# Layer 1 of a retention and two-layer feed-forward kernel: four directly multiplied weight blocks instead of eight, six pairs by seven products instead of four

## The chip, the cores and the metric

One Trainium2 chip, one core. The metric is the device time of one execution in microseconds (us), and lower is better. MB and GB/s count 10^6 and 10^9 bytes; the KB of the profile's DMA lists are 1024 bytes.

## The reference

Retention (attention with a decaying mask and no softmax) over 4 batches, 8 heads, 576 positions and 64 dimensions a head, then two feed-forward layers on the 2304 x 512 result:

```python
ret = scale * (q @ k.T) * Dmat          # Dmat = gamma ** (i - j) for i >= j, else 0
x = merge_heads(ret @ v)                # 2304 tokens x 512
h = x @ w_in;  g = h * cos(h);  x = g @ w_out                       # layer 1
h = x @ w2_in; g = max(h, 0) + log1p(exp(-abs(h))); y = g @ w2_out  # layer 2
```

w_in is 512 x 2048 and w_out 2048 x 512. The weights come as 64-bit words and are turned into float32 on the chip. Every float32 product is done as three matmuls of a high and a low part (high x high, high x low, low x high).

## The kernel before, in words

A weight block is 128 of the 2048 hidden features, so a layer has 16 (`NF`). A pair is two of them.

**Retention.** 32 pieces (`front`, `masks`, `states`, `back`, `after`), one for a head pair and a part of a batch. The first 16 run alone, the other 16 are spread over the first three token groups of layer 1 (`SPREAD`). Their results x are kept in SBUF as high and low parts and stored to DRAM (`xdh`, `xdl`).

**Layer 1, first part** (`moe_a`, `slot`, `out1`). Blocks 0 to `FA` - 1 have their weights resident (tiles `wh`, `wl`, made by `weight`). Tokens go in five groups (512, 512, 384, 384, 512 columns). For each group and block: 12 matmuls from x into a PSUM bank (L798), the activation h cos h on ScalarE and VectorE (`activate`), its two parts `gh` and `gl`, and 12 matmuls into four accumulators (L897). The partial result of a group goes to DRAM (`pd`).

**Layer 1, second part** (`quad`, `unit`). The other blocks are taken in pairs, over three chunks of 768 tokens, each two halves of 384 columns. A quad is one pair and one chunk: the product of two feature blocks, two halves of the model dimension and two halves of the tokens is done in seven products of 6 matmuls (L1002) on sums and differences of the operands, where straight multiplication takes eight. `x_load` makes the seven x operands of a chunk (three of them from sums on VectorE or GpSimd), `weight_in` the seven weight operands of a pair (tile `pair`). Bank copies (`cv`, `c5`) and adds on VectorE put the seven products together. A `unit` is the output product of one pair and one half chunk: 24 matmuls (L1353). After a pair's last unit GpSimd adds the result to `pd` in DRAM by an accumulating DMA.

**Layer 2** (phases 1 and 2 of the loop over `ph`) is done in pairs throughout, four pairs a phase; its out product too goes by seven products (`unit_s`, L1131). Its in-weights stand in two slots: a pair is made from the converted weights (`wd` in DRAM) for the first chunk, stored to `wpd`, and read back for the others (`weight_in_s`). The chunks run through the pairs forwards and backwards by turns (`turn`), so that two pairs need no load.

**Weights.** `convert` loads one block's half (512 KB), and ScalarE and VectorE turn it into float32. `convert_ahead` stores the result to `wd`; `load_values` and `weight_in_s` read it.

**The order of the work.** Nothing is ordered on the chip. Every operation is handed to `Plan` with an engine, a planned duration and a key (the time at which it is wanted). `Plan.order` picks, again and again, the operation that can start first on its engine (ties by key), lets some operations go to one of two engines, and so fixes one order for each engine. The some 40 constants at the top move keys. All loads and stores but the accumulating ones are issued by SyncE (SP in the profile), in one order: a DMA whose buffer is not ready holds up those behind it.

## Time and profile before

| | |
|---|---|
| median of 3 runs (lowest, highest) | 843.84 us (843.11, 844.63) |
| the profiled execution, its span | 841.66 us, 839.9 us |
| busy TensorE (PE), VectorE (DVE), ScalarE (ACT), GpSimd (POOL) | 98%, 77%, 65%, 9% of the span |
| granted TensorE clock | full in all 40 slices of the page |
| DMA | 174.69 MB, 208 GB/s over the span |

The page gives busy times of engines; a matmul's own duration is longer than its share of the time, because matmuls overlap. What a matmul costs in a dense stretch is the distance between starts, which the chain of waits shows.

### The profile page before, as it was taken

Reading aid. Unit: us, or ns where it says so; the run is one execution under the profiler, and the core shown is the slowest. Engines: PE = TensorE matmul, PEld = TensorE weight load, DVE = VectorE, ACT = ScalarE, POOL = GpSimd, SP = SyncE. Lnnn points to the kernel's source line nnn. Section 1 sums busy time; section 2 is a strip of 40 time slices with the busy share of each in tenths; the row PEclk is TensorE's granted clock in tenths of the full one; section 3 lists DMA queues with packets and bytes.
Section 4 is the critical chain, followed back from the end, with each engine's and each line's share of the span. In section 5 each row is a group of like instructions: output and inputs, shape, how many; then the busy total and the mean of one; then the engine's idle time right before and its main releaser. Section 6 shows DMA issues by size and latency. Waiting matters only on the chain.

```text
span 839.9 us, 15626 instructions
## 1 busy us (share of the span) xinstructions
PE 824.0 (98%) x5732; PEld 773.7 (92%) x5732; DVE 649.5 (77%) x1441; ACT 548.2 (65%) x1189; POOL 72.6 (9%) x94
## 2 busy tenths in 40 slices
PE   7999999999999999999999999999999999999996
PEld 5767877899988999999999998999999999999996
DVE  3789765655894798769877689779698998876786
ACT  1379664756875888879987675564565765555442
POOL 3531000100021000111011010000000000000000
PEclk9999999999999999999999999999999999999999
DMA  9698878747594134776787477617477683555222
GB/s 318 263 361 267 310 251 284 252 142 235 158 325 134 64 113 151 201 225 196 202 245 266 122 223 267 224 65 262 151 248 274 237 309 139 189 207 201 88 76 76
DMA packets 67292, 174.69 MB, mean 208 GB/s; under 512 B 6160, under 2 KB 28560, under 8 KB 65168
## 3 DMA queue, kind: packets, MB, share of 16 engines
q1 hardware_dynamic: 63760, 168.98, 57.2%
q0 software_dynamic: 3456, 4.72, 3.8%
q8 instruction: 45, 0.74, 0.3%
q14 instruction: 31, 0.25, 0.1%
HBM read 110.76 MB, written 62.91 MB: 207 GB/s over the span
## 4 chain that ended last, share of the span: by engine, by line
PE 88%; DVE 6%; DMA 2%; issue 2%; ACT 1%; SPq 0%; POOL 0%; DVEq 0%; POOLq 0%; ACTq 0%
PE acc L1131 19%; PE ha L1002 16%; PE acc L897 12%; PE acc L1353 11%; PE s L1002 8%; PE hb L798 4%; PE ha L798 4%; PE hb L1002 4%; PE o L711 2%; DMA raw<-in_qkv 1%; PE o L798 1%; PE s L798 1%; PE s L634 1%; DVE x L314 1%; DMA dq_t<-in_dq 1%
## 5 line engine op out<-in xcount | busy, mean ns | idle before, releaser
L1002 PE MATMUL ha<-x,pair 128*128 128x384 f32 x864 | 174.7, 336 | 1.2 <-ACT cv L318 0.6
L1002 PEld LDWEIGHTS ha<-x,pair 128*128 128x128 f32 x864 | 149.4, 188 | 3.7 <-DVE x L314 1.2
L1131 PE MATMUL acc<-pair,gh 128*128 128x256 f32 x576 | 113.3, 283 | 0.0
L1353 PE MATMUL acc<-gh,pair 128*128 128x384 f32 x384 | 105.5, 335 | 0.0
L1131 PEld LDWEIGHTS acc<-pair,gh 128*128 128x128 f32 x576 | 89.5, 191 | 0.5 <-ACT gh L1112 0.3
L1131 PE MATMUL acc<-pair,ah 128*128 128x256 f32 x432 | 86.7, 282 | 0.5 <-DVE pt L1210 0.5
L1002 PE MATMUL s<-x,pair 128*128 128x384 f32 x432 | 86.8, 335 | 0.0
L1131 PE MATMUL acc<-pair,gl 128*128 128x256 f32 x288 | 81.7, 284 | 0.7 <-DVE gl L314 0.7
L1002 PEld LDWEIGHTS s<-x,pair 128*128 128x128 f32 x432 | 75.6, 188 | 0.4 <-DVE pair L314 0.2
L1131 PEld LDWEIGHTS acc<-pair,ah 128*128 128x128 f32 x432 | 70.0, 190 | 0.7 <-DVE pt L1210 0.7
L1353 PEld LDWEIGHTS acc<-gh,pair 128*128 128x128 f32 x384 | 70.1, 188 | 0.3 <-ACT pt L318 0.2
L1353 PE MATMUL acc<-gl,pair 128*128 128x384 f32 x192 | 64.1, 334 | 0.0
L1131 PE MATMUL acc<-pair,al 128*128 128x256 f32 x216 | 61.1, 283 | 0.3 <-DVE al L314 0.3
L897 PE MATMUL acc<-gh,wh 128*128 128x512 f32 (+1 forms) x160 | 60.2, 377 | 0.3 <-ACT gh L876 0.3
L897 PE MATMUL acc<-gl,wh 128*128 128x512 f32 (+1 forms) x160 | 59.1, 369 | 0.3 <-DVE gl L314 0.3
L897 PE MATMUL acc<-gh,wl 128*128 128x512 f32 (+1 forms) x160 | 58.9, 368 | 0.0
L841 ACT ACTIVATE er<-er 128x384 f32<-128x384 f32 (+1 forms) x88 | 48.3, 551 | 16.2 <-DVE er L837 15.8
L847 ACT ACTIVATE er<-er,hp_t 128x384 f32<-128x384 f32 (+1 forms) x88 | 56.4, 641 | 1.1
L1131 PEld LDWEIGHTS acc<-pair,gl 128*128 128x128 f32 x288 | 55.0, 191 | 1.5 <-DVE gl L314 1.5
L1112 ACT ACTIVATE gh<-sf 128x512 fp32r<-128x512 f32 x72 | 45.3, 632 | 16.3 <-DVE sf L1086 7.5
L318 ACT ACTIVATE cv<-ha 128x384 f32<-128x384 f32 x72 | 35.4, 491 | 31.5 <-PE ha L1002 31.0
L314 DVE TENSOR_TENSOR gl<-sf,gh 128x512 fp32r<-128x512 f32 x72 | 49.5, 689 | 6.4 <-ACT gh L1112 4.8
(215 smaller groups left out, 1851.1 us busy)
## 6 DMA issues: line engine op xcount, KB each, us to landing
wr<-in_w SPq DMA_DIRECT2D x64, 512.0 KB, 4.9
wpd<-pair SPq DMA_DIRECT2D x8, 1792.0 KB, 6.9
pair<-wpd SPq DMA_DIRECT2D x8, 1792.0 KB, 6.9
wd<-wk SPq DMA_DIRECT2D x40, 256.0 KB, 2.8
sd<-x SPq DMA_DIRECT2D x12, 768.0 KB, 3.7
x<-sd SPq DMA_DIRECT2D x12, 768.0 KB, 6.4
raw<-in_qkv SPq DMA_DIRECT2D x12, 640.0 KB, 6.3
x<-pd SPq DMA_DIRECT2D x18, 384.0 KB, 5.1
```

The costliest lines, as they stand in the source:

```text
L314: e.tensor_tensor(out_, a, hi.bitcast(F32), ALU.subtract)
L318: nc.scalar.activation(out_, in_, AF.Copy)
L634: nc.tensor.matmul(X()[j][:, z], k_(j, z), q_(z)[Z[j]], start=True, stop=True)
L711: nc.tensor.matmul(o_at(z)[Z[j]], lhs(j), rhs(j), start=start, stop=stop, skip_group_check=True)
L798: nc.tensor.matmul(h_[:, 0:n], lhs, rhs[:, d, 0:n], start=(k == 0), stop=(k == 3 * NC - 1))
L841: nc.scalar.activation(e["r"], e["r"], AF.Abs)
L847: nc.scalar.activation(e["r"], e["r"], AF.Sin, bias=hp_t[:, 0:1], scale=-1.0)
L897: nc.tensor.matmul(acc[o][:, 0:n], l[:, s], e[r], start=(first and z == 0), stop=(last and z == 2))
L1002: nc.tensor.matmul(R(r), w_(a), x_(b), start=(start and n == 0), stop=(n == 5), skip_group_check=True)
L1112: nc.scalar.activation(T[hk], T[fk], AF.Copy)
L1131: nc.tensor.matmul(acc[m][:, i * 256:i * 256 + 256], l[p], r[o], start=(s == 0 and i == 0 and n == 0), stop=(s == half_p - 1 and n == 2), ...
L1353: nc.tensor.matmul(acc[m][:, 0:HN], l[:, z_], e[r], start=(first and z == 0), stop=(last and z == 2))
```

## The change

The first part keeps four blocks (`FA` 8 to 4). The second part has six pairs (`P0`), numbered from `FQ[0]` = 2. Their in-weights use the two-slot ring that layer 2 had, now in a pool of its own (`pp`): for the first chunk a pair is made from `wd` and stored to `wpd`, and later chunks read it back. So all twelve of these blocks are converted ahead and stored, where two pairs were converted in place before. The last token group's four blocks (`moe_a(NM - 1, job)`, spaced by `OFF`) are laid among the first quads. Product operands and groups are the same in both layers now. `c5` is gone: the copy of product 5 goes into the first half of `cv`, and `cv` has one buffer instead of two. `weight_in` is removed; other tiles move between pools. The constants are other numbers.

```diff
-FA = 8
+FA = 4
-FS = 5
+FS = 2
...
-XHOME = "qqqqrrrpp"
+XHOME = "qqqqqqqpp"
...
+    pp = pool("pp", 1, side="right")
-    wpd = dram.tile([128, 8, 3584], F32, name="wpd")
+    wpd = dram.tile([128, NF, 3584], F32, name="wpd")
...
-    MB = t_ + 1.0
+    P0 = (NF - FA) // 2
+    NQ = (P0, half_p, half_p)
+    FQ = (FA // 2, 0, half_p)
-    CM = [MB - TIE]
+    CM = [M[-1] - TIE]
+    MB = M[-1] + OFF[-1] + LL + 6.0
     for ph in range(3):
-        CM.append(CM[-1] + nb * half_p * UC[ph])
+        CM.append(CM[-1] + nb * NQ[ph] * UC[ph])
...
-        q = turn(y, s) + (ph - 1) * half_p if ph else half_p + s
+        q = FQ[ph] + turn(ph, y, s)
...
-                if name == "5":
-                    c["5"] = wp["q"].tile([128, HN], F32, tag="c5", name="c5", bufs=2)
-                elif z == 0:
-                    c["v"] = wp["q"].tile([128, 2, HN], F32, tag="cv", name="cv", bufs=2)
-                copy(eng, c["5"] if name == "5" else c["v"][:, z], R(r))
+                if name != "5" and z == 0:
+                    c["v"] = wp["q"].tile([128, 2, HN], F32, tag="cv", name="cv", bufs=1)
+                copy(eng, c["v"][:, z], R(r))
...
-        op(ACT_DVE, both, K + 3 * DT - EARLY, keep(3, 0, "5"), r=[rk[3], ("qopen",)], w=[(c5,)], new=[("c5", 2, c5)])
+        op(ACT_DVE, both, K + 3 * DT - EARLY, keep(3, 0, "5"), r=[rk[3], ("qopen",)], w=[(cv, 0)])
...
-            nc.vector.tensor_tensor(R(4), R(1), c["5"], ALU.add)
+            nc.vector.tensor_tensor(R(4), R(1), c["v"][:, 0], ALU.add)
...
-        key = KI(ph, y, s) - (W[0] if y == 0 and s < 2 else W[1])
+        key = KI(ph, y, s) - (W[0] if y == 0 and s < 2 else W[1] if y == 0 or ph else XW)
         def make():
-            p = wp[HOME[slot_]].tile([128, 3584], F32R, tag=f"pair{slot_}", name="pair")
+            p = pp.tile([128, 3584], F32R, tag=f"pair{slot_}", name="pair")
...
-    for i, (layer, q) in enumerate([(1, half_p + 2), (1, half_p + 3)] + [(2, q) for q in range(half_p)]):
-        convert_ahead(layer, q, M[1] + CA[0] + 4 * i * CA[2], CA[2])
-    for q in range(2):
-        k = M[NM - 2] + W2[0] + W2[1] * q
-        job(k, weight_in, 1, half_p + q, k, W2[3], False)
-        job(k + 0.1, weight_out, 1, half_p + q, k + 2 * W2[3], W2[3], False)
+    moe_a(NM - 1, job)
+    for i in range(P0):
+        k = M[0] + CA[0] + 4 * i * CA[2]
+        job(k, convert_ahead, 1, FQ[0] + i, k, CA[2])
+    for q in range(NP2):
+        k = CM[0] + CA[1] + 4 * q * CA[3]
+        job(k, convert_ahead, 2, q, k, CA[3])
```

The orders, read from the two programs. In them and in the trace, `x` is an operand of a chunk or a group, `pair` a pair's weights, `wr` the raw words of a block's half, `wk` its float32 value, `raw` the input of a retention piece, and `acc` an accumulator; a number behind a name is a buffer. In the changed program the helper of all SP rows has line 309 (306 before), the first part's products L757 and L856 (L798 and L897 before), the quads' L963 (L1002 before).

TensorE before, where the first quad begins (`x_2435` and `x_2438` are operands of the first chunk, `pair_2433` is the first pair's weights, `acc2` and `acc3` belong to the last token group):

```order
L897 MATMUL acc2_2998<-gh_3107,wl_1000 128x512
L897 MATMUL acc3_3026<-gh_3107,wh_999 128x512
L897 MATMUL acc3_3026<-gl_3110,wh_999 128x512
L897 MATMUL acc3_3026<-gh_3107,wl_1000 128x512
L1002 MATMUL ha_3167<-x_2435,pair_2433 128x384 x6
L1002 MATMUL hb_3187<-x_2438,pair_2433 128x384 x6
L897 MATMUL acc0_2983<-gh_3144,wh_1043 128x512
```

Two products of the quad stand together, and after them the last group goes on. By then the first part lacks only the out products of the last group's last three blocks.

TensorE in the change, at the same quad (`x_1955` to `x_1961` are the first chunk's seven operands, `pair_129` the first pair's weights, `x_1542` the last group's x):

```order
L856 MATMUL acc2_2007<-gh_2040,wl_794 128x384
L963 MATMUL ha_2087<-x_1955,pair_129 128x384 x6
L856 MATMUL acc3_2100<-gh_1934,wh_707 128x384
...
L757 MATMUL o_2166<-x_1542,wh_707 128x512 x2
L757 MATMUL o_2166<-x_1542,wl_708 128x512
L963 MATMUL hb_2186<-x_1958,pair_129 128x384 x6
L963 MATMUL s_2199<-x_1956,pair_129 128x384 x6
L963 MATMUL ha_2087<-x_1959,pair_129 128x384 x6
L963 MATMUL s_2199<-x_1957,pair_129 128x384 x6
L963 MATMUL ha_2087<-x_1960,pair_129 128x384 x6
L856 MATMUL acc0_2251<-gh_2240,wh_707 128x512
```

One product stands alone, then come 38 rows of the first part (30 of the fourth group, the first product of the last group), then five products in a row. The last group, which was almost done before, has only begun here.

SyncE before, where the first chunk's operands are loaded:

```order
L306 DMA wr2_2742<-in_w1 128x1024
L306 DMA wr0_2762<-in_w1 128x1024
L306 DMA xdh_95<-x_1355 512x1x384
L306 DMA xdl_96<-x_1355 512x1x384
L306 DMA wr1_2802<-in_w1 128x1024
L306 DMA x_2435<-xdh_95 128x2x384
L306 DMA x_2435<-xdl_96 128x2x384
L306 DMA x_2436<-xdh_95 128x2x384
L306 DMA x_2436<-xdl_96 128x2x384
```

SyncE in the change, where the first chunk's operands are loaded:

```order
L309 DMA wr0_1916<-in_w1 128x1024
L309 DMA wd_103<-wk_1930 128x512
L309 DMA x_1955<-xdh_98 128x2x384
L309 DMA x_1955<-xdl_99 128x2x384
L309 DMA x_1956<-xdh_98 128x2x384
L309 DMA x_1956<-xdl_99 128x2x384
...
L309 DMA x_1958<-xdh_98 128x2x384
L309 DMA x_1958<-xdl_99 128x2x384
L309 DMA wr1_2037<-in_w1 128x1024
L309 DMA wpd_104<-pair_129 128x3584
L309 DMA wpd_104<-pair_130 128x3584
```

The loads follow raw words and converted halves directly, as before, and behind them come the stores of the first two pairs' seven operands (1.84 MB each), which were not there.

SyncE in the change, at the fourth pair of the second part (`pair_2495`); nothing like it stands in this stretch of the order before:

```order
L309 DMA wr2_2386<-in_w1 128x1024
L309 DMA wd_103<-wk_2425 128x512
L309 DMA wr_2453<-wd_103 128x2x512
L309 DMA wpd_104<-pair_2287 128x3584
L309 DMA pair_2495<-wd_103 128x512
L309 DMA pair_2495<-wd_103 128x2x256
L309 DMA wd_103<-wk_2499 128x512
L309 DMA wr_2525<-wd_103 128x2x512
L309 DMA wd_103<-wk_2527 128x512
L309 DMA wr_2542<-wd_103 128x2x512
L309 DMA wr_2560<-wd_103 128x2x512
```

The load of the fourth pair's weights stands behind the store of the third pair's, which waits for that pair's operands to be made, and behind all that was issued before: by the shapes of the rows 67.1 MB through the second load of `pair_2495`. Over the whole program SP issues 203.0 MB in the change and 169.0 MB before; TensorE has 288 matmuls of 512 columns where it had 576, and 2820 of 384 where it had 2472.

## Rows read from the trace of the kernel before

**Rows 1.** The page, its head and section 1: busy us, share of the span.

```profile
span 839.9 us, 15626 instructions
...
PE 824.0 (98%) x5732; PEld 773.7 (92%) x5732; DVE 649.5 (77%) x1441; ACT 548.2 (65%) x1189; POOL 72.6 (9%) x94
```

**Rows 2.** Waits of TensorE, whole span: us in total, times, longest us.

```profile
PE acc L639 <- POOL raw L604: 2.8, 2, 2.3
PE hb L1388 <- DVE er L1380: 1.5, 1, 1.5
PE s L634 <- DVE st L693: 1.0, 1, 1.0
...
PE ha L1002 <- ACT cv L318: 0.6, 1, 0.6
```

**Rows 3.** The chain of waits: start us, us, what.

```profile
62.66 2.72 PE ha L798 x12
...
168.33 2.08 PE ha L798 x12
...
345.54 4.16 PE acc L1353 x24
```

**Rows 4.** Timeline of TensorE: first block's product, then first quad's; start us, us.

```profile
48.96 0.72 PE L798 MATMUL ha<-x,wh 128*128 128x512 f32 x2
...
273.91 1.23 PE L1002 MATMUL ha<-x,pair 128*128 128x384 f32 x6
```

**Rows 5.** Windows: busy time of each engine, clock, DMA's busy share and rate.

```profile
core 0: us, PE busy (x) PEld busy (x) DVE busy (x) ACT busy (x) POOL busy (x), PEclk, DMA share, GB/s
0.00:45.00 45.00, 39.70 (x590) 29.99 (x592) 25.45 (x89) 10.66 (x34) 20.51 (x37) 1.00 0.81 299
45.00:115.00 70.00, 68.44 (x466) 54.26 (x462) 57.89 (x121) 58.52 (x116) 12.58 (x16) 1.00 0.87 309
45.00:190.00 145.00, 143.44 (x1047) 116.87 (x1042) 100.89 (x219) 103.43 (x210) 19.83 (x26) 1.00 0.75 264
50.00:60.00 10.00, 9.39 (x79) 6.70 (x78) 8.93 (x18) 9.24 (x20) 4.15 (x5) 1.00 1.02 411
220.00:240.00 20.00, 20.00 (x113) 19.49 (x112) 19.60 (x38) 16.98 (x33) 2.78 (x3) 1.00 0.68 233
560.00:600.00 40.00, 40.00 (x287) 40.00 (x286) 33.84 (x76) 22.20 (x54) 0.00 (x0) 1.00 0.51 188
```

**Rows 6.** ACT and DVE by line and shape: busy us, mean ns of one, idle before.

```profile
L1228 ACT ACTIVATE pair<-tt 128x768 fp32r<-128x768 f32 x8 | 6.8, 846 | 0.1
L1251 DVE TENSOR_TENSOR tt<-pair 128x256 f32<-128x256 f32 x24 | 9.5, 418 | 0.0
L314 DVE TENSOR_TENSOR pair<-tt,pair 128x768 fp32r<-128x768 f32 x8 | 7.6, 954 | 0.3
L318 ACT ACTIVATE c<-s 128x384 f32<-128x384 f32 x36 | 17.6, 490 | 4.1 <-PE s L1002 3.9
L1025 DVE TENSOR_TENSOR hb<-hb,cv 128x384 f32<-128x384 f32 x36 | 20.2, 562 | 5.2 <-ACT cv L318 3.1 <-ACT gh L876 1.0 <-PE hb L1002 0.9
```

**Rows 7.** DMA of the page: issues, KB each, median us from issue to landing.

```profile
wpd<-pair SPq DMA_DIRECT2D x8, 1792.0 KB, 6.9
pair<-wpd SPq DMA_DIRECT2D x8, 1792.0 KB, 6.9
```

**Rows 8.** Timeline of SP: two reads of the ring in layer 2.

```profile
521.09 0.32 SPq L306 DMA_DIRECT2D pair<-wpd  x1
...
535.23 0.32 SPq L306 DMA_DIRECT2D pair<-wpd  x1
```

More of the change, by code (lines that the diff above doesn't have):

```diff
@@ L512, in weight_out @@
-    def weight_out(layer, q, key, step, ahead):
-        slot_ = q % half_p
-        wk = ("wo", layer, q)
-        made = (wk, "made")
-        def make():
-            p = wp[HOME[slot_]].tile([128, 2048], F32R, tag=f"po{slot_}", name="pair")
+            p = wp[POH[slot_]].tile([128, 2048], F32R, tag=f"po{slot_}", name="pair")
             T[wk] = p.rearrange("p (j g d) -> p j g d", j=2, g=2)
-        op("host", 0.0, key, make, r=[(HOME[slot_] + "open",)], w=[made], new=[(f"wo{slot_}", 1, wk)])
-        if ahead:
-            oks, ovs = load_values(layer, q, 1, key)
+        op("host", 0.0, key, make, r=[(POH[slot_] + "open",)], w=[made], new=[(f"wo{slot_}", 1, wk)])
@@ L524, in weight_out @@
+        oks, ovs = load_values(1, q, 1, key)
         for j in range(2):
-            k = key + j * step
-            ok, ov = (oks[j], ovs[j]) if ahead else convert(layer, 2 * q + j, 1, k)
+            k = key + j * W3[4]
+            ok, ov = oks[j], ovs[j]
             op("act", t_act(512), k + 2.2, lambda j=j, ov=ov: nc.scalar.activation(T[wk][:, j, 0], ov(), AF.Copy),
@@ L1043, in made @@
                 if gk not in T:
-                    a = place(half_p * y + s, t, j)
-                    T[gk] = stash()[:, a:a + HN]
+                    n = P0 * y + s
+                    a = place(n, j)
+                    T[gk] = stash()[:, a:a + HN] if t else first_g(n, j)
                 return T[gk]
@@ L1300, in make @@
         def make():
-            if s < 2:
-                p = wp[HOME[2 + s]].tile([128, 3584], F32R, tag=f"pair{2 + s}", name="pair")
+            if s == 0:
+                p = wp["q"].tile([128, 3584], F32R, tag="ox", name="pair")
                 T[wk] = p[:, 0:1792], p[:, 1792:3584]
             else:
-                z = 2 * s - 4
-                T[wk] = tuple(wp[HOME[z + g]].tile([128, 2048], F32R, tag=f"po{z + g}", name="pair")[:, 0:1792] for g in range(2))
-        op("host", 0.0, key, make, w=[made], new=[(f"wp{2 + s}", 1, wk)] if s < 2 else [(f"wo{2 * s - 4 + g}", 1, wk) for g in range(2)])
+                z = 2 * s - 2
+                T[wk] = tuple(wp[POH[z + g]].tile([128, 2048], F32R, tag=f"po{z + g}", name="pair")[:, 0:1792] for g in range(2))
+        i_ = op("host", 0.0, key, make, w=[made], new=[(f"wo{2 * s - 2 + g}", 1, wk) for g in range(2)] if s else [("ox", 1, wk)])
+        if ph == 1 and s == 0:
+            first_out.append(i_)
         r_, t_ = (lambda i: (i, False)), (lambda i: (i, True))
@@ L1344, in unit @@
                 ak = ("acc", 0, y, t, m)
-                first, last = s == 0 and j == 0, s == half_p - 1 and j == 1
+                first, last = s == 0 and j == 0, s == P0 - 1 and j == 1
                 def mo(m=m, j=j, e=e, first=first, last=last):
@@ L1578, in retention_moe_moe @@
             job(k, x_load, ph, y, k)
-            for s in range(half_p):
+            for s in range(NQ[ph]):
                 job(KI(ph, y, s), quad, ph, y, s)
+                job(KI(ph, y, s) - max(0.1, W[0] if y == 0 and s < 2 else W[1] if y == 0 or ph else XW), weight_in_s, ph, y, s)
                 if not ph:
@@ L1608, in retention_moe_moe @@
             plan.ops[i][4].update(plan.users[last_wr[2]])
-        for t in range(2):
+        for n in range(P0, nb * P0):
             for j in range(2):
-                for s in range(half_p):
-                    a = place(half_p * (nb - 1) + s, t, j)
-                    if a < 512 * m + 512 and a + HN > 512 * m:
-                        plan.ops[i][4].update(plan.users[gof(0, nb - 1, s, t, j)])
+                a = place(n, j)
+                if a < 512 * m + 512 and a + HN > 512 * m:
+                    plan.ops[i][4].update(plan.users[gof(0, n // P0, n % P0, 1, j)])
+    for i in first_out:
+        for n in range(P0, nb * P0):
+            for j in range(2):
+                plan.ops[i][4].update(plan.users[gof(0, n // P0, n % P0, 0, j)])
     plan.emit(nc)
```

224 lines of the change are left out of this document (96 added, 128 removed).

## The prediction

> **What bounds the kernel now.** I read the engines' busy time first: TensorE is busy for 824.0 us of 839.9 [rows 1]. Then its waits: the longest in total is 2.8 us, the ones on the second part's bank copies 0.6 us [rows 2], so what TensorE has to do sets the time, and the other engines and the DMA queues lie beside it. A change that takes work from TensorE gains just that, as long as nothing else becomes late. So there are two questions: how much work goes, and whether what feeds TensorE still comes in time where it is moved together.
>
> **What TensorE saves.** In a dense stretch 12 matmuls of 512 columns take 2.72 us, so one takes 0.2267 us; 12 of 384 columns take 2.08 us and 24 take 4.16 us, 0.1733 us each, in the first part and in the second [rows 3]. Four blocks leave the first part. By the two orders that is 288 matmuls of 512 columns and 192 of 384: 65.3 + 33.3 = 98.6 us. Two pairs come into the second part, three chunks each: 2 x 3 x (42 + 48) = 540 matmuls of 384 columns, 93.6 us. The saving is **5.0 us**. It is less than the 36 spared products' 6.2 us, since the second part uses 384 columns at 0.451 ns a column where groups of 512 cost 0.443. The 32 retention pieces and all of layer 2 keep their matmuls.
>
> **What comes onto the other engines.** Six pairs instead of four give 6 quads more, with 18 copies on ScalarE and 18 adds on VectorE; four blocks less give 20 activations less against the 24 of the new quads. VectorE has 1486 instructions for 1441, ScalarE 1211 for 1187. Over the span neither matters at 77% and 65% [rows 1]. It matters where they come together. The busiest 20 us of VectorE before were 19.60 us of 20, and TensorE lost nothing there [rows 5]. In the change, from the first block of the fourth group to the first product of the fourth pair, TensorE has 228 matmuls of 384 and 96 of 512 columns and a piece and a half of retention, some 65 us. VectorE has 124 instructions there. At 0.478 us (57.89 us for 121) to 0.516 us (19.60 us for 38) each [rows 5] they take 59 to 64 us. That fits, barely. Before, the stretch from 45 to 115 us, with VectorE at 57.89 of 70 us and ScalarE at 58.52, cost TensorE 1.56 us [rows 5]. I bound this term at 0 to 3 us, twice that, and take 0, the busiest window being the nearer case; its cover is gone if VectorE also has to wait for loads.
>
> The shared buffer adds a wait. Product 5's copy now waits for the add that reads the first copy; behind the copy wait product 3, which writes the same bank, and so TensorE. From product 2's end to product 3's start there are two products, 2.08 us; the add takes 0.56 us and the copy 0.49 us [rows 6], which leaves 1.03 us. If the add finds VectorE in an operation of 768 columns (0.95 us), nothing is left for the signals between engines. I take 0, since the order puts the adds early, and at most 0.1 us in each of 18 quads, 2 us; a gain is excluded, since a wait is only added.
>
> The ring of two costs nothing by itself: layer 2 runs on it before, reads of 1.84 MB are 14 us apart there [rows 8] and land 6.9 us after issue [rows 7], and TensorE is busy for 40.00 of 40 us [rows 5]. A quad with its two units takes 42 + 48 matmuls, 15.6 us, so the second part gives as much room.
>
> **What comes onto the DMA queue, the uncertain term.** SP issues 203.0 MB instead of 169.0 over the span: six pairs' operands are stored and eight times read back, 14 x 1.84 MB, and four pairs' halves go through DRAM. More important is when. Before, TensorE starts its first block at 48.96 us and its first quad at 273.91 us [rows 4]; between them lie 540 matmuls of 512 and 384 of 384 columns, 189.0 us, so 36.0 us are retention and small losses. The same 36.0 us stand in the change, whose order is the same up to that first block. Its first quad then starts at 48.96 + 36.0 + 192 x 0.2267 + 162 x 0.1733 = 156.6 us. The fourth pair's first product comes after 288 and 318 matmuls, at **205.3 us**. Its operands were loaded at most some 4 us before: three sums of 0.42 us and the pass of 768 columns on ScalarE (0.85) and VectorE (0.95) are 3.1 us [rows 6], the rest waits for a turn. So the load must land by 201.3 us. In SP's order 67.1 MB stand up to and with that load. By 45 us, 45 x 299 GB/s = 13.5 MB had been moved [rows 5], by rows that are the same in both programs up to 11 MB. So **53.6 MB in 156 us, 343 GB/s without a pause.** The second chunk's first operands ask for the same: 83.6 MB by 250 us.
>
> The queue before never had to do that. From 45 to 115 us it moved 309 GB/s at a share of 0.87, from 45 to 190 us 264 at 0.75 [rows 5]: 352 to 355 GB/s of busy time. Raw words and inputs alone went at 411 [rows 5]. At 355 GB/s without a pause the load lands at 196 us and nothing is late. At 309, the rate of the best long stretch, it lands at 218.5 us and the quad is 17.2 us late. Between these I take 338 GB/s, 0.96 of 352, nearer to the upper end, because the pauses before were a queue with nothing to send, and now there is always something behind: landing at 203.6 us, **2.3 us late**. By the same rate the second chunk's operands land at 252.4 us, 2.3 us late again, which the first delay already covers. Later the demand falls: the first read-back, 89.1 MB, is wanted at 281 us, 320 GB/s.
>
> The Trainium skill, page "DMA: Bandwidth & Descriptors", section "Bandwidth", gives 425 GB/s for one core alone with 16 MB in one transfer and 341 with 1 MB, measured on loads issued from GpSimd. With 425 the load would land at 171 us and all 5.0 us would be kept; with 341 it would land at 202.2 us, 0.9 us late. This trace has 411 GB/s for large reads and 352 for the mixture, so I go by the trace.
>
> **The sum.** -5.0 + 2.3 + 0 + 0 = -2.7 us. The profiled execution took 841.66 us, so 839.0 us for one like it; the median of the runs, 843.84, stands 2.2 us above it, and from that the prediction is **841.1 us**. 0.2% is 1.7 us, about what a measurement of this kernel can tell.
>
> **Rivals.**
> *The DMA queue sets the pace of layer 1's start (slower).* The place is the load of the fourth pair, then the second chunk's operands. For it: 343 GB/s are wanted for 156 us, within 3% of the best mixed rate, and SP issues in order, so one store that waits holds up all loads. Also, writes and short rows have a larger part than before. Against it: the load has 4 us to spare at the rate of the busy time. It decides from 332 GB/s on, where the delay eats all 5.0 us. At 320 GB/s the delay is 11.2 us and the time 850 us, at 309 it is 17.2 us and 856 us.
> *Nothing is late (faster by all of it).* For it: at 352 GB/s the load is in time, and the ring has worked in layer 2. Against it: a queue with no pause for 156 us, which no stretch shows. The time is 843.8 - 5.0 = 838.8 us; if part of the 1.56 us that TensorE lost around 45 to 115 us goes too, 838.
> *Given back in small pieces (no change).* VectorE at 59 to 64 of 65 us, the shared buffer and the queue take 3.3 to 6.7 us together: 842.1 to 845.5 us. For it: three resources are nearly full in the same 60 us. Against it: VectorE at 98% cost nothing before.
>
> **How the numbers follow.** The forecast, with 1 to 3.3 us given back, gets 0.33, nothing late 0.14, the small pieces 0.20, the DMA bound 0.33. So faster 0.47, same 0.20, slower 0.33. The range starts at 838, where all is kept and a little more, and goes to 851, beyond the 850 us of 320 GB/s; that leaves out some 0.04 below and 0.12 above. The likeliest side's own range is 838 to 842.1.
>
> **What would show it.** Right: 5206 matmuls with the counts above; the first quad near 156 us and the fourth pair's first product within 3 us of 205; the DMA share over 0.93 from 45 to 200 us; waits of TensorE on pair or x of some 2 us in the quads' first chunk; later none on `cv`. Wrong: TensorE idle by over 5 us between 150 and 260 us with DMA or a late operand as releaser, which is the first rival; or waits on VectorE of some us in the fourth and last groups; or many short waits of product 3 on the copy, which would make the shared buffer the cost; or dense matmuls at another distance, which would upset the 5.0 us.

## The result and the profile after

Over 12 runs the changed kernel takes 846.67 us (845.19 to 848.93); the kernel before took 842.12 us in 12 runs beside it. The ratio is 1.0054, 95% interval 1.0041 to 1.0067: **0.54% slower**, some 4.5 us. The forecast was 2.7 us faster. The profiled execution (`after` below), 848.93 us, is the longest of the twelve, so a repetition of the same kernel (`again`, profiled at 846.07 us) is used for the accounts below. Lines of the changed program: L757 and L856 the first part's products, L963 the quads', L317 the subtractions, L321 the bank copies.

The page after, its head and section 1:

```profile
span 846.8 us, 15943 instructions
...
PE 825.4 (97%) x5792; PEld 783.1 (92%) x5792; DVE 666.9 (79%) x1486; ACT 550.7 (65%) x1213; POOL 84.1 (10%) x105
```

TensorE has less to do, yet is busy for 825.4 us here and 823.3 in `again`, against 824.0 before [rows 1], in a longer span. The dense distances have not changed; the chain of waits after (start us, us, what) has the same 2.72, 2.08 and 4.16 us as [rows 3]:

```profile
106.20 2.72 PE hb L757 x12
...
115.81 2.08 PE hb L757 x12
...
277.93 4.16 PE acc L1318 x24
```

Waits of TensorE after, whole span (us in total, times, longest us):

```profile
PE acc L598 <- POOL raw L563: 2.4, 2, 1.7
PE s L593 <- DVE st L652: 2.3, 1, 2.3
PE ha L963 <- DVE g L809: 2.1, 2, 1.1
PE acc L856 <- ACT gh L835: 1.9, 1, 1.9
...
PE acc L856 <- DVE gl L317: 1.2, 3, 0.8
PE ha L963 <- ACT cv L321: 1.2, 2, 0.6
PE ha L963 <- DVE pair L317: 0.6, 1, 0.6
```

The wait on `st` was 1.0 us before [rows 2]; the ones on g, gh, gl and pair are new or longer, and there are two on `cv` for one. None of these is on a DMA. Windows after, with the columns of [rows 5]:

```profile
45.00:115.00 70.00, 67.41 (x549) 51.98 (x546) 54.10 (x127) 46.30 (x96) 13.64 (x18) 0.98 0.89 317
45.00:205.00 160.00, 154.55 (x1158) 128.91 (x1155) 127.07 (x281) 106.56 (x226) 28.95 (x32) 0.98 0.93 335
150.00:300.00 150.00, 144.92 (x786) 136.38 (x783) 127.07 (x224) 124.40 (x257) 28.85 (x26) 0.99 0.90 316
```

From 45 to 205 us the queue moved 335 GB/s at a share of 0.93; the forecast was 338 and over 0.93. From 150 to 300 us TensorE stands still for 5.1 us, though VectorE is busy for 85% of that stretch and ScalarE for 83%.

**Where the time went.** Take the start of each TensorE row and subtract the dense time of all matmuls of 512, 384 and 256 columns ahead of it (their number times 0.2267 or 0.1733 us, and 0.1195 us, the distance of layer 2's 256-column matmuls in the timelines). What is left is retention and what TensorE has lost up to there. At the last row it is 94.14 us before and 103.76 in `again`, 9.6 us more. The dense time is 739.54 us before and 734.56 in the change, so the saving is 5.0 us as forecast. The span ends 5.99 us after the last row's start, and 6.22 us before the change, which is another 0.2 us saved. Stretch by stretch, `again` against the kernel before:

| stretch of TensorE's rows | lost in addition |
|---|---|
| up to the first block (50.66 us, before 48.96) | 1.7 us |
| from there to the first quad (158.21 us, before 273.91) | 0.0 us |
| the first chunk's quads and the first part's rows among them, up to the second chunk's first product (260.23 us, before 325.95) | 8.3 us |
| the second and third chunk, to their last product (444.12 us, before 447.77) | -0.9 us |
| the first quad of layer 2 with the way into it (to 472.7 us, before 476.8) | 3.7 us |
| the rest of layer 2 | -3.2 us |

-5.0 - 0.2 + 9.6 = +4.4 us, which is 844.3 against 839.9. Of the 8.3 us, 6.3 are lost before the fourth pair's first product. `again` has pauses of 1.87, 0.81, 0.58, 0.58 and 0.96 us at 162, 177, 204, 206 and 250 us, 4.8 us together; counted by starts, these five places cost 5.7 us. Why the kernel before loses 3.2 us more in the rest of layer 2 was not followed up.

### The profile page after: what moved, and what is told of

Read it like the earlier page. It is cut to its first block, busy times and chain, and to the rows that moved or that the text cites. A ratio compares the mean times of both kernels' runs of the same rounds, so it can differ in the third digit from the quotient of the medians.

```text
span 846.8 us, 15943 instructions
## 1 busy us (share of the span) xinstructions
PE 825.4 (97%) x5792; PEld 783.1 (92%) x5792; DVE 666.9 (79%) x1486; ACT 550.7 (65%) x1213; POOL 84.1 (10%) x105
## 4 chain that ended last, share of the span: by engine, by line
PE 68%; issue 17%; DVE 6%; DMA 4%; ACT 3%; POOL 1%; SPq 0%; POOLq 0%; DVEq 0%; ACTq 0%
PE acc L1092 20%; PE ha L963 15%; PE s L963 8%; PE acc L1318 7%; PE acc L856 4%; PE hb L963 4%; PE o L670 2%; PE ha L757 1%; DMA raw<-in_qkv 1%; PE hb L757 1%; POOL pd L1337 1%; PE s L593 1%; DMA pd<-pt 1%; DVE gl L317 1%; DVE pair L317 1%
## 5 line engine op out<-in xcount | busy, mean ns | idle before, releaser
L963 PE MATMUL ha<-x,pair 128*128 128x384 f32 x1008 | 203.7, 336 | 3.9 <-DVE g L809 2.1
L963 PEld LDWEIGHTS ha<-x,pair 128*128 128x128 f32 x1008 | 174.4, 188 | 7.2 <-DVE g L809 2.7
L1318 PE MATMUL acc<-gh,pair 128*128 128x384 f32 x576 | 157.1, 335 | 0.6 <-ACT pt L321 0.6
L1318 PEld LDWEIGHTS acc<-gh,pair 128*128 128x128 f32 x576 | 105.0, 188 | 1.0 <-ACT pt L321 0.9
L963 PE MATMUL s<-x,pair 128*128 128x384 f32 x504 | 101.3, 335 | 0.1
L1318 PE MATMUL acc<-gl,pair 128*128 128x384 f32 x288 | 96.3, 334 | 0.0
L963 PEld LDWEIGHTS s<-x,pair 128*128 128x128 f32 x504 | 88.2, 188 | 1.2 <-ACT cv L321 0.4
L321 ACT ACTIVATE cv<-ha 128x384 f32<-128x384 f32 x84 | 41.1, 489 | 30.7 <-PE ha L963 30.1
L317 DVE TENSOR_TENSOR gl<-sf,gh 128x512 fp32r<-128x512 f32 x72 | 49.4, 689 | 8.1 <-ACT gh L1073 6.5
L1318 PEld LDWEIGHTS acc<-gl,pair 128*128 128x128 f32 x288 | 54.1, 188 | 0.1
L963 PE MATMUL hb<-x,pair 128*128 128x384 f32 x252 | 50.7, 335 | 0.0
L1062 ACT ACTIVATE ah<-gs 128x384 fp32r<-128x384 f32 x60 | 31.5, 525 | 28.5 <-PE acc L1092 28.3
```

The costliest lines, as they stand in the source:

```text
L317: e.tensor_tensor(out_, a, hi.bitcast(F32), ALU.subtract)
L321: nc.scalar.activation(out_, in_, AF.Copy)
L963: nc.tensor.matmul(R(r), w_(a), x_(b), start=(start and n == 0), stop=(n == 5), skip_group_check=True)
L1062: nc.scalar.activation(A_(0), T[uk][:, 0:HN], AF.Copy)
L1318: nc.tensor.matmul(acc[m][:, 0:HN], l[:, z_], e[r], start=(first and z == 0), stop=(last and z == 2))
```

## How the pauses come about

**At 164 us** (162 us in `again`). Timeline after, all engines, cut to the rows of this chain (start us, us, engine, line, what, the idle time before and its releaser):

```profile
157.81 1.84 POOL L1471 TENSOR_TENSOR tt<-x 128x768 f32<-128x768 f32 x1
158.31 2.15 DVE L317 TENSOR_TENSOR pair<-tt,pair 128x768 fp32r<-128x768 f32 x1
...
161.33 0.55 DVE L809 TENSOR_TENSOR s<-s,er 128x384 f32<-128x384 f32 x1
...
161.79 0.54 DVE L796 SCALAR_TENSOR_TENSOR er<-ek,o 128x384 f32<-128x384 int32 x1
...
162.37 0.52 ACT L800 ACTIVATE er<-er 128x384 f32<-128x384 f32 x1 [1.80 <-DVE er L796]
162.80 0.47 ACT L321 ACTIVATE cv<-ha 128x384 f32<-128x384 f32 x1
...
163.17 0.60 ACT L806 ACTIVATE er<-er,hp_t 128x384 f32<-128x384 f32 x1
...
163.67 0.48 ACT L835 ACTIVATE gh<-s 128x384 fp32r<-128x384 f32 x1
...
164.20 0.44 PE L856 MATMUL acc<-gh,wh 128*128 128x384 f32 x1 [1.87 <-ACT gh L835]
```

VectorE has the second pair's 768 columns to subtract, 0.95 us before [rows 6], and takes 2.15 beside GpSimd's sum. So the two activations behind it come late. ScalarE then stands idle for 1.80 us with the next activation's steps at its head; `gh<-s`, for which TensorE waits and whose input is ready at 161.9 us, stands behind them. Neither engine is short of time: the written order puts a late chain in front of the one that TensorE needs.

**At 204 and 206 us.** Timeline of TensorE and ScalarE in `again`:

```profile
202.49 1.20 PE L963 MATMUL ha<-x,pair 128*128 128x384 f32 x6
...
203.73 0.49 ACT L321 ACTIVATE cv<-ha 128x384 f32<-128x384 f32 x1
...
204.28 1.34 PE L963 MATMUL ha<-x,pair 128*128 128x384 f32 x6 [0.58 <-ACT cv L321]
...
205.65 0.49 ACT L321 ACTIVATE cv<-ha 128x384 f32<-128x384 f32 x1 [0.30 <-PE ha L963]
...
206.20 1.34 PE L963 MATMUL ha<-x,pair 128*128 128x384 f32 x6 [0.58 <-ACT cv L321]
```

Three products follow one another in the bank `ha`, with a copy of it between each two. The distance is 1.79 and 1.92 us instead of 1.04.

**At the start.** Timeline of VectorE and TensorE in `again`, before the first block:

```profile
45.65 0.69 DVE L403 SCALAR_TENSOR_TENSOR wk<-wy,wr 128x512 int32<-128x512 int32 x1 [0.41 <-ACT wy L391]
46.26 0.95 DVE L317 TENSOR_TENSOR wl<-wk,wh 128x512 fp32r<-128x512 f32 x1
...
47.84 0.28 DVE L652 SCALAR_TENSOR_TENSOR st<-st,dk_t,s 128x64 f32<-128x64 f32 x1
...
48.17 0.37 PE L593 MATMUL s<-raw 64*128 64x128 f32 x1 [2.32 <-DVE st L652]
```

Two conversion steps of weights stand ahead of the state that TensorE waits for; before, the wait was 1.0 us [rows 2]. The 1.7 us are those of one execution: in the twelve traces with the same order up to there the first block starts between 49.35 (`short_feed`) and 53.24 us (`short_both`), in three of the kernel before between 48.96 and 49.83.

**The clock.** Windows of `again`, the start and then the entry into layer 2:

```profile
45.00:50.00 5.00, 2.68 (x44) 2.02 (x40) 4.53 (x14) 4.46 (x13) 2.14 (x3) 0.92 0.74 233
50.00:55.00 5.00, 5.00 (x26) 3.63 (x24) 3.36 (x9) 2.75 (x6) 0.00 (x0) 0.74 0.97 336
...
445.00:450.00 5.00, 3.85 (x22) 3.53 (x22) 5.00 (x12) 4.98 (x10) 0.00 (x0) 1.00 0.28 107
450.00:455.00 5.00, 4.35 (x17) 4.03 (x17) 3.30 (x7) 3.97 (x9) 1.06 (x2) 0.69 0.60 202
```

The same windows before, at the start:

```profile
45.00:50.00 5.00, 4.04 (x60) 3.16 (x56) 4.57 (x17) 3.58 (x12) 1.87 (x3) 1.00 0.94 351
50.00:55.00 5.00, 5.00 (x42) 3.73 (x41) 4.44 (x9) 4.50 (x10) 1.89 (x3) 1.00 1.01 410
```

Windows after, at 165 us and at the entry into layer 2:

```profile
165.00:170.00 5.00, 5.00 (x21) 5.00 (x21) 4.38 (x7) 2.10 (x4) 0.48 (x1) 0.66 1.03 438
...
450.00:455.00 5.00, 3.21 (x17) 2.57 (x16) 4.91 (x12) 4.97 (x10) 0.00 (x0) 1.00 0.54 174
```

Behind some of the pauses the granted clock is 0.66 to 0.74 for a few us (1.2 of 2.4 GHz for a part of them). `after` and `again` are one program, and its clock fell at other places: at 166 us in `after` alone, at 452 us in `again` alone. By the account above TensorE loses 7.8 us in `after` and 6.4 in `again` from the first quad to the first part's last row, and 1.9 and 2.6 us in layer 2's first quad. So a fall cost some 1.3 us at the one place and 0.7 at the other. Each run lists its mean clock: 18 runs of the change have 0.995 on average, 99 of the kernel before 0.9975. Among the 18, the four at 0.992 and 0.993 have a mean span of 846.2 us, the seven at 0.996 and more 843.6. A line through them falls by 0.53 us for each 0.001; by that, some 1.4 of the 4.5 us go with the clock.

## The experiments

All edit the changed kernel, but for the two on the kernel before. "Order unchanged" means that every instruction keeps its place.

**start**: the start constants of before.

```diff
-W0 = (46.735, 4.788, -1.046)
+W0 = (45.931, 4.788, 4.772)
```

> The change at 846.7 us with W0's first and third number of the kernel before (45.931 and 4.772 for 46.735 and -1.046): the out half of each resident block is converted 4.8 us after its in half, not ahead of it, so fewer conversions stand on VectorE between the last lone retention pieces. Theory A (VectorE is late at the stage's starts, and the pauses are made longer by the clock that falls after them): the first block starts at 49 to 50 us, not 52.8, and the time falls by 2 to 4 us, to 842.7 to 844.7. Theory B (the DMA queue is late in the first 200 us): a start that is earlier by 3 us is lost again at the quads, 846 to 847. If the 3.8 us at the start were chance of one execution: 846.7.

852.19 us against 841.58, 1.0120 (1.0103 to 1.0138). The first block starts at 48.60 us, 2 us earlier than in `again`, but the rest of the order comes out differently and loses more at the quads. A constant can't be tried alone here; the next edits therefore keep the order.

**pair2**: the second pair's weights wanted 15.6 us later, so that not two pairs are made at once.

```diff
+P2 = 18.0
...
+        W = (P2,) + W[1:] if s == 1 and not ph else W
...
```

> The change with the second pair of layer 1 made 15.6 us later (its key 18.0 us ahead of its quad, not 33.6), so that its eight VectorE operations (4.1 us) stand behind the activations of the fourth group's last blocks. Theory A: the wait of 1.9 us on gh at 164 us goes, and the stretch at 0.66 of the clock behind it (1.7 us); time down by 2 to 4 us, to 842.7 to 844.7. Theory B: the same bytes in nearly the same order, the second pair's load later: 846.7 to 848. Theory C (the shared copy buffer costs): 846.7, and the two waits of 0.6 us on cv near 208 us stay.

858.67 us, 1.0211 (1.0179 to 1.0242). The pause at 164 us goes; others come, among them 0.94 us at 173, 1.25 at 209, 1.58 at 270 and 1.77 at 274 us, and the clock falls to 0.56 to 0.76 from 270 to 280 us.

**short_bits** and **short_conv** (order unchanged): a conversion step of the paired blocks' weights on 32 of 512 columns, in the first on VectorE alone, in the second one on ScalarE too. The other columns leave it out, so these weights are others.

```diff
-            a = T["wk", u]
+            c = 32 if layer == 1 else 512
+            a = T["wk", u][:, 0:c]
...
+            c = 32 if layer == 1 and f >= FA else 512
+            nc.scalar.activation(y[:, 0:c], T["wr", u][:, 0:c, 1].bitcast(F32), AF.Prelu, scale=2.0 ** -112, alpha=2.0 ** 32)
...
```

> The change in the same order of instructions, but the second pass of the conversion of layer 1's twelve paired blocks (wk<-wr,wk, 24 times 0.69 us) covers 32 of 512 columns, so the lowest three bits of these weights are left out; VectorE has some 13 us less to do between 55 and 190 us, and no transfer changes. Theory A: the waits on gh, gl and g between 150 and 260 us shrink; time down by 3 to 7 us, to 840 to 844. Theory B (bytes bound): 846 to 847.5, since the bytes and their order are the same.

> The change in the same order, with ScalarE's and VectorE's passes of the conversion of layer 1's paired blocks on 32 of 512 columns (24 x 0.6 us less on each), so these weights are others. ScalarE is busy for 4.7 to 5.0 of 5 us in several stretches from 190 to 245 us. Theory A2 (ScalarE's throughput there is the cost): time down by 2 to 5 us, 842 to 845. Theories B and D: 845.5 to 847, as when VectorE alone had less.

846.27 us, 1.0057 (1.0036 to 1.0078), and 847.79 us, 1.0068 (1.0049 to 1.0086). VectorE has 656.3 and 655.9 us for 666.9, ScalarE 541.3 for 550.7 in the second, and the five pauses stay as they were to 0.05 us. How much VectorE and ScalarE have to do in all is not what TensorE waits for.

**two_stores** and **short_stores** (order unchanged): each of layer 1's six pairs stored twice, 11.0 MB more; or only its first 128 of 3584 words a row, 10.6 MB less (the rest isn't stored, and the read-backs of the same size take x from DRAM, so they don't give the weights).

```diff
+            if not ph:
+                nc.sync.dma_start(wpe[:, s], T[wk, "all"].bitcast(F32))
```

```diff
-        dma(lambda: wpd[:, zd], lambda: T[wk, "all"].bitcast(F32), ...
+        dma(lambda: wpd[:, zd, 0:some], lambda: T[wk, "all"][:, 0:some].bitcast(F32), ...
```

> The change in the same order, but each pair's seven operands of layer 1 are stored twice, the second time to memory that nobody reads: 6 x 1.84 MB more, 5.5 MB of them ahead of the fourth pair's load, 16 us of queue at 338 GB/s. Theory B: the fourth pair, and with it TensorE, comes 10 to 16 us later: 857 to 863 us, a wait of TensorE on pair or x of that size. Theory A: the queue has slack, TensorE loses at most 2 us: 846 to 849.

> The change in the same order, but of each pair's operands of layer 1 only 128 of 3584 columns are stored, and the read-backs take their 1.84 MB from the stored x: 6 x 1.77 MB less to store, 5.3 MB of them ahead of the fourth pair's load, 16 us of queue at 338 GB/s (the later chunks of layer 1 multiply other numbers). Theory B (the queue is late in the change itself, as it was by 13 us with 11 MB more): time down by 3 to 8 us, 839 to 844. Theory D (the queue is near its edge but in time; what is lost between 150 and 260 us is the latency of short chains, products of a quad that follow each other in one bank with nothing else to do between): down by at most 1 us, 845.5 to 847, and the waits on gh, gl, cv and g stay.

Twice: 859.92 us, 1.0212 (1.0194 to 1.0230), 13 us more than the change. Now TensorE does wait for the queue (timeline of `two_stores`; `pt` is the buffer of the store to `pd`):

```profile
183.42 0.80 PE L857 MATMUL acc<-gh,wh 128*128 128x512 f32 x1 [2.92 <-ACT pt L322]
...
217.59 1.31 PE L964 MATMUL s<-x,pair 128*128 128x384 f32 x6 [1.25 <-DMA wd<-wk]
```

Less: 847.57 us, 1.0061 (1.0040 to 1.0082), no gain, with the same pauses (1.87, 0.78, 0.58, 0.58, 0.97). So the queue does not limit the change as it stands, and with 11 MB more TensorE waits for it.

**fill** (order unchanged): eight matmuls without use in the pause at 164 us, to keep the clock up.

```diff
...
+                            nc.tensor.matmul(b, hi[:, 0:128], hi[:, 0:512], start=(z == 0), stop=(z == 7))
```

> The change in the same order, with eight matmuls of 512 columns (1.8 us) into an idle bank ahead of the output product that waits 1.9 us for gh at 164 us; they add nothing to the result. If the clock falls to half because of that pause: the stretch at 0.66 behind it goes, and the time falls by 1 to 1.7 us, to 845 to 845.7. If the fall has another reason, or the pause is not always there: 846.7 to 848.5.

846.84 us, 1.0054 (1.0041 to 1.0067). The clock was 1.00 behind that pause here, but also in other runs without the edit, `again` among them. The run settles nothing on the clock.

**own_c5**: product 5's copy in a buffer of its own, as before the change.

```diff
+                c["5"] = c["v"][:, 0] if ph else first_g(-1, 0)
...
-            nc.vector.tensor_tensor(R(4), R(1), c["v"][:, 0], ALU.add)
+            nc.vector.tensor_tensor(R(4), R(1), c["5"], ALU.add)
```

> The change in the same order, with the copy of product 5 in a buffer of its own in layer 1 (a free part of the tile of the first half's results). Theory C (the shared buffer is what costs): the two waits of 0.6 us on cv near 208 us go, time down by 1 to 2 us, to 845. Theory D: those waits come from three products of a quad in one bank with nothing between; 846.7, and they stay.

846.22 us, 1.0055 (1.0039 to 1.0070), with the two pauses of 0.58 us on `cv` still there. They come from the bank, not from the shared buffer.

**move164, moves, moves2**: single instructions placed elsewhere by hand, nothing else. `move164` puts `gh<-s` and its `gl` ahead of the late activation's steps. `moves` and `moves2` do that too, and move one or two instructions at the start, one at 180 us and four at 252 us; `moves` also five at the entry into layer 2, so that 14 and 10 are moved. The numbers are those of the operations in the plan: what, beside which, before (0) or behind (1).

```diff
-        for i in self.order():
+        seq = self.order()
+        for i, j, after in ((691, 672, 1), (700, 691, 1), (692, 843, 0)):
+            seq.remove(i)
+            seq.insert(seq.index(j) + after, i)
...
+        for i in seq:
```

> The change with three of these instructions moved: on ScalarE gh of the block in s ahead of the other block's step, on VectorE its gl ahead of an x sum. Theory D: the pause at 164 us falls from 2.0 to 0.8 us, all others stay, and the time falls by 1 to 2 us, to 844.7 to 845.7. If it comes back: 846.7.

> The change with thirteen instructions of VectorE and ScalarE moved by a few places, all else as it was (TensorE, GpSimd, SP, every byte and every duration): the part of wk behind the masks ahead of the first block; gh and gl of the block in s ahead of the other block's steps (164 us); gl ahead of an x operand (179 us); the steps that free bank ha ahead of conversions and of gl (252 us); the pair's sums ahead of gs at the phase change (453 us). Theory D (what is lost are pauses that the written order makes: one instruction that stands behind others which nobody waits for): the pauses of 2.3, 2.0, 0.8, 0.95 and 1.8 us fall to some 1.0, 0.8, 0.2, 0.2 and 1.3, and the time falls by 3.5 to 5 us, to 841.7 to 843.2. If what lies behind the pauses is late as well, they come back a few products later: 845.5 to 847.

> The change with eleven instructions moved: those of the run before without the ones at the phase change (which did not help there), and at the start the copy st<-s on ScalarE ahead of a conversion step, since there the state waited for ScalarE. Theory D: the pause at the start falls from 2.3 to some 1.2 us, those at 164, 179 and 252 us to 0.6, 0.2 and 0; 2 to 3.5 us less than the change beside it, 843 to 844.7 where the change takes 846.7. Against it: 0 to 1 us less, the rest comes back later.

> The change itself once more, on the chip of the run above, for a comparison side by side: 846 to 847.5 us, pauses of 2.3, 2.0, 0.8, 1.2, 0.95 and 1.8 us at the same products. The first block at 49.6 to 50.5 us (a start at 52.8 us, as in the first profile, would mean that its 3 us are no chance).

847.23 us, 1.0063 (1.0041 to 1.0085); 845.51 us, 1.0033 (1.0016 to 1.0050); 845.63 us, 1.0046 (1.0034 to 1.0059); and `again`, the change itself beside `moves2`, 846.92 us, 1.0064 (1.0050 to 1.0079). With `move164` the pause of 1.87 us becomes three of 0.67 us in all, and 0.35 us is waited a few us on. In `moves2` 0.66 us is left at 159 to 163 us, then come 0.35, 0.23 and 0.38 up to 176 us. TensorE gets through one place and waits for the same late work at the next: from the first quad to the first part's last row it loses 6.5 us in all three, 6.4 in `again`. At 250 us it is otherwise. The pause of 0.96 us is gone in both `moves` and `moves2`, and by the account above the 0.9 us stay gained to the end of layer 1. In the times this can't be told from the clock: the 16 runs of the two have 0.997, and on the line through the change's own runs their mean span of 843.7 us is what the change has at that clock.

**short_chain** and **chain_before** (orders unchanged): two steps of each of layer 1's activations, absolute value and sine, on 32 columns, in the change and in the kernel before; the other columns leave them out. **short_both** adds the short stores.

```diff
-                    nc.scalar.activation(e["r"], e["r"], AF.Abs)
+                    nc.scalar.activation(e["r"][:, 0:32], e["r"][:, 0:32], AF.Abs)
...
```

> The change with abs and sin of layer 1's activations done on 32 of the tile's columns instead of 384 or 512; the other columns leave these two steps out. Every instruction stands in its place. Two steps of each activation's chain become some 0.3 to 0.4 us shorter each. Theory D (TensorE's pauses are the length of the chain product, activation, product, at places where the written order leaves nothing between): the pauses at 164, 180 and 453 us, which wait on gh, gl and g, shrink by 0.5 us or more each, the two of 0.58 us on cv near 208 us stay unless ha comes free earlier; the time falls by 2.5 to 4 us, to some 842.5 to 844. Theory T (VectorE and ScalarE have too much to do there, or the queue is slow): no change, as when 24 passes of conversion were cut from 0.9 to 0.3 us each on both engines without effect: 846 to 847.

> The kernel before with the same edit: abs and sin of layer 1's activations on 32 columns, the other columns leave them out. Theory D: before had some 2.2 us of such pauses around its first quads and 1 us where its first block begins, so it gains 0 to 1.5 us, less than the change does. If it gains as much as the change does, the activations' length costs both kernels alike and says nothing on the difference between them.

> The short activations of short_chain and at once the short stores of short_stores (10.6 MB less on the queue in layer 1; a pair's stored operands but their first 128 words are left out). If the shorter chains let TensorE come earlier to the fourth pair, whose load had some 4 us to spare, theory Q (the queue is what would bind next) expects this 1 us or more below short_chain. Theory D alone expects the same time as short_chain within 0.5 us.

846.30 us, 1.0046 (1.0031 to 1.0061); 840.83 us, 0.9981 (0.9970 to 0.9992); 847.55 us, 1.0051 (1.0034 to 1.0068). The pauses at 162 and 250 us shrink by 0.6 us each, but a new one of 1.35 us on a quad's add comes at 242 us. From the first quad to the end of layer 1's quads TensorE loses 9.6 us, as in `again`. The median of the kernel before falls by 1.4 us (842.22 to 840.83, beside it). The length of the activations does not make the difference; the short stores again give nothing.

**short_feed** and **feed_before** (orders unchanged): the same, and in layer 1's quads the copies of the banks `ha` and `s` for the sums, and the adds on `hb` and `s`, on 32 of 384 columns; the other columns leave them out.

```diff
-                copy(eng, c["v"][:, z], R(r))
+                copy(eng, c["v"][:, z] if name == "5" else c["v"][:, z, 0:w32], ...
...
-        op("dve", ..., lambda: nc.vector.tensor_tensor(R(2), R(2), c["v"][:, 0], ALU.add), ...
+        op("dve", ..., lambda: nc.vector.tensor_tensor(R(2)[:, 0:w32], R(2)[:, 0:w32], c["v"][:, 0, 0:w32], ALU.add), ...
```

> The change with the short activations of short_chain and, in layer 1's quads, the copies cv and the adds on banks hb and s done on 32 of 384 columns (product 5's copy and the sum into the fourth bank stay whole; the other columns leave these steps out). Order unchanged. Theory D (pauses are latency of what stands between two products): the two pauses of 0.58 us near 205 us shrink to 0.2 or 0.3 us, and about as much goes in the other quads of layer 1; with short_chain's gain the time is 1.5 to 3 us below the change, 844 to 845.5. Theory O (the place of the work in the written order, not its length, sets the pauses): what one step saves is waited for at the next, and the time is that of short_chain, 846.3, within 0.5 us.

> The kernel before with the same two edits. It has 12 quads in layer 1 where the change has 18. Theory D: it gains less than the change does, 0 to 0.5 us more than chain_before's 1.4, so that the change's deficit of 4.6 us falls to 3.5 or less. Theory O: the deficit stays at 4.6 to 5.5 us.

**843.14 us**, 1.0015 (1.0001 to 1.0030), and 840.78 us, 0.9983 (0.9972 to 0.9995). The medians fall by 3.2 us in the change (846.30 to 843.14) and by nothing in the kernel before (840.83 to 840.78), and the intervals of `short_chain` and `short_feed` do not overlap. Not all of the 3.2 us is the work of the copies and adds: the mean clock of these runs is 0.9932 in `short_chain` and 0.9957 in `short_feed`, which on the line above is 1.3 us, and whether the edit raised it is not shown. The two profiled runs tell what happens where the edit acts. From the first quad to the end of layer 1's quads TensorE loses 9.6 us in `short_chain` and 8.9 in `short_feed`, although the clock is down to 0.74 from 160 to 165 us in the second alone, and such a fall cost some 1.3 us there in `after`. In the kernel before the same stretch falls from 2.0 to 1.3 us. So the copies and adds are worth some 2 us in the change and 0.7 in the kernel before, and 1.3 us of the difference. In the timeline of `short_feed` the two pauses on the bank `ha` are half as long, because the copy takes 0.20 us for 0.49:

```profile
202.93 0.20 ACT L321 ACTIVATE cv<-ha 128x32 f32<-128x32 f32 x1 [0.35 <-PE ha L963]
...
203.18 1.33 PE L963 MATMUL ha<-x,pair 128*128 128x384 f32 x6 [0.29 <-ACT cv L321]
...
204.80 1.32 PE L963 MATMUL ha<-x,pair 128*128 128x384 f32 x6 [0.29 <-ACT cv L321]
```

With both edits the change's median is 2.4 us behind that of the kernel before (843.14 to 840.78) instead of some 4.5, the clock's part included.

**start_order**: on VectorE one `wl<-wk,wh` placed behind the state at the start, on ScalarE `st<-s` two places earlier; nothing else.

```diff
+        for i, j, after in ((269, 234, 0), (219, 270, 1)):
```

> The change, with two instructions placed elsewhere and nothing else: on VectorE one subtraction wl<-wk,wh of 512 columns goes behind the state update st (L652) that TensorE waits for at 48 us, on ScalarE the copy st<-s goes ahead of two conversion passes. The pause of 2.32 us there becomes some 1.5 us. Theory C (a long enough pause costs twice, since TensorE then runs at a lower granted clock): the stretch from 50 to 55 us keeps clock 1.00 where it had 0.66 to 0.74, the mean clock of the runs rises from 0.995 to 0.996 or more, and the time falls by 1.5 to 2.3 us, to some 844.5 to 845.3. Without such a cost: 0.8 us, to 846.

846.89 us, 1.0054 (1.0036 to 1.0071). In its profiled run the pause is 1.48 us, the first block starts at 48.74 us and the clock stays full there (windows of `start_order`):

```profile
45.00:50.00 5.00, 3.52 (x41) 2.64 (x38) 4.47 (x15) 4.51 (x16) 1.60 (x3) 1.00 0.77 255
50.00:55.00 5.00, 5.00 (x42) 3.73 (x41) 4.46 (x10) 3.57 (x8) 1.35 (x2) 1.00 0.90 341
```

That run, 844.61 us, is the fastest of the six; the median does not move, nor do the mean clock (0.9953 for 0.9948) and the mean span (844.6 for 844.9) by more than their scatter. Theory C's 1.5 us are not there. The clock's share above is a relation among runs: two traces of one program show what a fall costs, but no edit has shown that a shorter pause prevents one.

## Why the prediction was wrong, point by point

- **The saving of 5.0 us was right**: 739.54 us of dense time became 734.56, with the dense distances as they were.
- **"The same 36.0 us stand in the change, whose order is the same up to that first block"** failed. From the first block to the first quad the 36.0 us are there (0.0 us lost in addition), but the first block comes 1.7 us later in `again`. The order is the same for TensorE's rows alone: VectorE and ScalarE have other rows ahead of the state update.
- **The DMA term, 2.3 us late, was 0**, and the first rival with it. The rate was forecast well (338 GB/s, 335 measured), but the first quads lose time before the load matters: the fourth pair's first product came at 213.45 us instead of 205.3. Timeline of `again`, TensorE:

```profile
213.45 1.20 PE L963 MATMUL hb<-x,pair 128*128 128x384 f32 x6
```

  and SyncE, the two loads for it:

```profile
198.14 1.61 SPq L309 DMA_DIRECT2D pair<-wd  x2
```

  They land 5.3 and 5.7 us after their issue, at 203.4 and 204.2 us; the prediction had 203.6. With its 4 us between load and product they were wanted at 209.4, so some 5 us were to spare. The queue came when it was forecast to come, and TensorE was not there yet; whether the 2.3 us would show in a kernel whose quads lose nothing, no run tells. With 10.6 MB less nothing is gained; with 11.0 MB more 13 us are lost.
- **"That fits, barely. [...] I bound this term at 0 to 3 us, twice that, and take 0, the busiest window being the nearer case"** is the step that failed most. The stretch of that sum, from the first block of the fourth group to the fourth pair's first product, in `again`:

```profile
140.35:213.45 73.10, 69.11 (x400) 61.34 (x399) 62.56 (x119) 55.82 (x116) 13.61 (x12) 1.00 0.91 337
```

  VectorE is busy for 62.56 us, within the 59 to 64 forecast, but the stretch takes 73.1 us and not 65. I compared VectorE's amount of work with the room for it. The amount does fit, and cutting it changed nothing (`short_bits`, `short_conv`). From the first quad to the fourth pair TensorE loses 6.4 us, over twice my upper bound, and the whole first chunk 8.3 us more than before. The rows show it waiting there for single late steps: an activation's output at 162 us, copies of one bank between its products at 204 and 206 us, an activation's product at 250 us. The busy window from 220 to 240 us [rows 5] told of room, not of chains. Runs show a part of this. Shorter copies and adds are worth some 1.3 us more in the change than in the kernel before, and with other places in the order the 0.9 us at 250 us go and stay away. The rest is read from the rows and not shown by an edit.
- **The shared buffer cost 0**, as forecast: `own_c5` changes nothing. The waits "of product 3 on the copy" come, but from the bank.
- **Layer 2** was not in the sum but for its matmuls. Its first quad and the way into it cost 3.7 us more than before, with VectorE at 5.00 and ScalarE at 4.98 of 5 us and, in `again`, a clock of 0.69 behind it; the rest of layer 2 loses 3.2 us less, so that 0.5 us remain.
- The corrected sum is -5.0 - 0.2 + 1.7 + 8.3 - 0.9 + 3.7 - 3.2 = +4.4 us. In mechanism the third rival, given back in small pieces, comes closest, but it allowed 6.7 us back where 9.4 came, and two of its three mechanisms, buffer and queue, had no part. That 846.67 us lies between 838 and 851 is luck: the upper end was set for the DMA rival, at 320 GB/s.

Open: most of the 6.4 us up to the fourth pair. The late subtraction beside GpSimd, which delays two activations at 158 us, is a candidate by the rows alone, since no run took GpSimd's sums away. How much of the 4.5 us is the clock is open too: 1.4 us by the line among runs, while the trace of `again` has two falls ahead of its last rows, that of `after` three and the profiled run of the kernel before none. No version was found that beats the kernel before: the best of those that compute the whole result, `moves`, is 0.33% behind it.

## What to carry to other kernels

When work is moved together, don't compare amounts with room; follow the chain from one product to the next that needs it, and count what the order puts between them: two products in one bank with a copy between stood 1.8 to 1.9 us apart here, for 1.04. A pause is a cause only if it doesn't come back elsewhere: taking 1.2 us from one left the time as it was. To tell length from amount, shorten a step to a few columns with every instruction in its place, and do the same to the kernel before. Where medians differ by 1 to 3 us, look at the granted clock of the runs as well, and at the stretch of the trace in which the edit acts.

## What was not expected of the hardware

- A subtraction on VectorE with two operands in SBUF took far longer beside a sum on GpSimd: 2.15 us for 0.95, and `gl<-g,gh` of 384 columns 1.93 us for 0.56 at 248 us. The subtraction at 158 us ends 0.81 us after GpSimd's sum, as if it had hardly begun before. A subtraction with one operand in a bank was not touched: 0.56 us at 164 us beside GpSimd's sum of 2.14 us (timeline after):

```profile
163.35 2.14 POOL L1471 TENSOR_TENSOR tt<-tt 128x768 f32<-128x768 f32 x1 [3.69 <-DVE tt L1471]
...
164.19 0.56 DVE L317 TENSOR_TENSOR gl<-s,gh 128x384 fp32r<-128x384 f32 x1 [0.38 <-ACT gh L835]
```

  The Trainium skill says so on the page "SBUF — State Buffer", section "Who interferes with whom": an instruction of VectorE with two inputs in SBUF contends with one of GpSimd that reads SBUF, and one of them waits for the other's end. This trace agrees with it, in both cases.
- The queue moved 374 GB/s from 150 to 200 us in `again`, at a share of 1.00, with loads, stores and read-backs mixed; I had taken 352 to 355 as what it can do with such a mixture.
